# Threshold attention with a squared-ReLU layer: squares of the first chunk on VectorE, its values in another PSUM bank, query copies a step earlier

## The chip, the cores and the metric

The kernel runs on one core of a Trainium2 chip. The metric is the device time in microseconds (us) of one execution, as the median of several runs. Five engines work side by side, each through its own queue in order: TensorE (PE, with its weight loads PEld), VectorE (DVE), ScalarE (ACT), GpSimd (POOL) and SyncE (SP), which here only issues DMAs. Semaphores order them against each other.

## What is computed

```python
scores = scale * np.matmul(q, k.transpose(0, 1, 3, 2))       # 8 batches x 8 heads, 576 x 576, head_dim 64
thresh = np.max(scores, axis=-1, keepdims=True) - tau
scores = np.where(scores >= thresh, scores, -1000000000.0)
attn = np.exp(scores - np.max(scores, axis=-1, keepdims=True))
attn = attn / (np.sum(attn, axis=-1, keepdims=True) + 1e-09)
x = np.matmul(attn, v)                                       # to (4608, 512), heads side by side
h = x @ w_in                                                 # (512, 2048)
r = np.maximum(h, 0.0)
out = (r * r) @ w_out                                        # (2048, 512)
```

Everything is fp32.

## The kernel before

**Visits and steps.** The attention is done by pairs of heads. A visit is a pair's walk over blocks of 128 query rows, one block to a step; the last block has only 64 rows, and its two heads lie side by side in one tile (`qmid`). The first batch is walked twice: visits 0 to 3 take blocks 0 and 1, visits 4 to 7 take blocks 2, 3 and 4, so that the first 256 tokens are complete early. Later visits take all five blocks.

In a step, TensorE makes scores into PSUM banks 0 to 3 (L280, for the last block L273 from `qmid`). VectorE takes row maxima (L317); ScalarE makes the bias and threshold (L340, L341) and the exponents (L343); VectorE applies the threshold and sums (L355), then makes a reciprocal (L359, L360); GpSimd divides (L365, L367). Two steps later TensorE transposes the weights (L414, L421, L427) in parts 0, 1 and 2, each into one of banks 4 and 5 in turn (`take("tx", (4, 5))`), and ScalarE copies them to `wT` (L415, L423, L428). Values are then made by `mix` (L530, from `wT` and `vs`, 20 matmul records), also into a bank of 4 and 5, and copied to `xT` (L513). At a visit's last step VectorE transposes the next visit's queries and keys (L254). `split_left` (L248) copies the last 64 queries of both heads into `qmid` on ScalarE: two copies of 64x64.

**Rounding of weights.** The weights of the second part arrive by DMA in 32 pieces of 128x512. Each piece passes through five instructions in stages: L149 and L150 on ScalarE, L152 and L154 on VectorE (integer `tensor_scalar`), L156 and then L158 on GpSimd, which writes the finished piece to `w_in_sb` or `wo` and lets the next load start (L136). This is spread over the steps up to about 200 us: one piece in most steps, two in a few.

**The second part.** Tokens are taken in chunks of 256. Chunk 0 is done plainly (`PLAIN = 1`): 16 pieces `mlp_in` (L577), two of which share a PSUM bank, and then `mlp_out` (L759). Later chunks use a scheme with fewer products (`product`, L794, and `unit`, L688). For the first layer of chunk 0, `take("mm", (6, 7))` gives banks 6 and 7 in turn, one to each pair of pieces. After a pair, `square` runs: ScalarE's relu from PSUM to `g` (L587), and GpSimd's multiplication of `g` by itself (L588).

**Order of the work.** Each engine's order is written out by the kernel's Python loop, not by a scheduler. `waiting` is the queue of pieces of the second part; `fill` puts as many into each quarter of a step as `rate` allots in estimated us, and `after` runs what a piece left to be done (`posts`) one or two calls later. Steps before `early_to` go through `early_step`; the steps around the change go through the loop at L1186 to L1294; there `split_left(n)` stands at L1231, in the visit's second step (`at == 1`), after the exponents. Its copies are read by the scores of the visit's last step. The 8 squares of chunk 0 run between 60 and 136 us, during visits 5 to 8. For visits 5 to 7 the three steps are here called first, second and third (blocks 2, 3 and 4).

```python
        if s in mixes and old:
            mix(*mixes[s])
...
        if old:
            turn(*old, 2)()
```

So values are made after parts 0 and 1 of the transposes, and part 2 comes after the values.

Of the kernel before, what the change touches and what calls it, by code (L numbers as in the profile page):

```python
# [12 lines left out]
ALU = mybir.AluOpType  # L13
# [6 lines left out]
def kernel(  # L20
# [10 lines left out]
    nc = tc.nc  # L31
# [14 lines left out]
    PLAIN, SEVEN = 1, 2  # L46
# [34 lines left out]
    at = RAW * 2 * WP  # L81
# [127 lines left out]
    def arrived(t):  # L209
        assert all(x[0].tensor.name != t.tensor.name for x in loads)  # L210
# [163 lines left out]
    def take(what, among):  # L374
        used[what] += 1
        at = among[used[what] % len(among)]
        if what == "mm":
            last_used(at)
        return bank[at]
# [8 lines left out]
    def last_used(x):  # L388
        oldest.remove(x)
        oldest.append(x)  # L390
# [10 lines left out]
    def place_of(n, i):  # L401

        return n % 2 * 4 + 2 * i if n < HP else n % 2 * 5 + 2 * (i - FIRST) if n < 2 * HP else 2 * i
# [123 lines left out]
    def mix(n, cols):  # L527

        def term(ps, u, c, at, rows=slice(0, P), first=False, last=False):
            nc.tensor.matmul(ps[u * D:(u + 1) * D, :], vs[n % 2][rows, u * (NBLK + 1) + c, :],  # L530
                             wT[rows, at // REST:(at + ps.shape[1]) // REST, NBLK if c == NBLK else u * (NBLK + 1) + c, :],
                             start=first, stop=last)

        above, below = slice(0, D), slice(D, P)
        arrived(vs[n % 2])
        if not by_dma(n):
            ps = take("tx", (4, 5, 6, 7) if early() else (4, 5))[:, 0:cols.stop - cols.start]
            at = place_of(n, cols.start // P) * REST
            for c in range(NBLK + 1):
                for u in range(2):  # L540
                    term(ps, u, c, at, first=(c == 0), last=(c == NBLK))
            put(n, cols.start, ps, False)
            return
        n1, n2 = 2 * P + REST, 2 * P
        at = ODD if paired(n) and n % 2 else ONE
        one, two = bank[0], bank[4]
        groups = (one[:, 0:n1], at, (above, below)), (two[:, 0:n2], TWO, (below, above))
        for ps, x, _ in groups:
            for c in range(NBLK):
                for u in range(2):  # L550
                    term(ps, u, c, x, first=(c == 0))

        for ps, x, places in groups:
            for u, rows in enumerate(places):
                term(ps, u, NBLK, x, rows, last=True)
        put(n, 0, one[:, ONE - at:ONE - at + 2 * P], True)
        left = ODD if at == ODD else LEFT - at
        put(n, NBLK * P, one[:, left:left + REST], False)
        put(n, 2 * P, two[:, 0:n2], True)
# [10 lines left out]
    def mlp_in(j, x):  # L570

        f, at = FORDER[x], j * TCH % RING
        if x % 2 == 0:
            used["h"] = take("mm", (6, 7)) if j < PLAIN else next_bank()
        h = used["h"].rearrange("p (f n) -> p f n", f=2)
        for c in range(NMC):
            nc.tensor.matmul(h[:, x % 2, :], w_in_sb[:, c, f * P:(f + 1) * P], xT[:, c, at:at + TCH],  # L577
                             start=(c == 0), stop=(c == NMC - 1))
        if x == NFT - 1:
            read_to["x"] = (j + 1) * TCH  # L580
            if j == SEVEN - 1:
                ask(*((j, "S3", q, c) for q in range(2) for c in range(2)))
        posts = [lambda: some_sums(1)] if j >= PLAIN else []
        if x % 2:
            def square():
                to = g[:, f - 1:f + 1, :]
                nc.scalar.activation(out=to, in_=h, func=AF.Relu)  # L587
                nc.gpsimd.tensor_tensor(out=to, in0=to, in1=to, op=ALU.mult)  # L588
                if j >= PLAIN and x % 8 == 7:
                    square_half(x // 8 * (HF // 2))  # L590
            posts.append(square)
        return posts
# [252 lines left out]
    def paired(n):  # L845

        return n >= 3 * HP
# [7 lines left out]
    def by_dma(n):  # L855

        return n >= 3 * HP - 1
# [7 lines left out]
    for s, (n, i) in enumerate(steps):  # L865
# [5 lines left out]
        if i in mixed:  # L871
            first, lag = mixed[i]
            cols = slice(first * P, S if by_dma(n) else min((i + 1) * P, S))
# [6 lines left out]
    chunk_at, j = {}, 0  # L880
# [9 lines left out]
    waiting = deque()  # L890
    state = {"us": 0.0, "left": 0.0, "step": 0, "free": False, "rounded": 0, "usable": 0, "then": [], "last": [], "made": 0}

    def early():
        return state["step"] < early_to
# [46 lines left out]
    def after():  # L941
        now = state["last"]
        state["last"] = []
        for fn in state["then"]:
            state["last"] += fn() or []
        state["then"] = []
        for fn in now:
            fn()
# [237 lines left out]
    for s in range(END + 1):  # L1186
        state["step"] = s
        if early():
            rounded_by.append(state["rounded"])
            done += pieces[s]  # L1190
            early_step(s)
            continue
        if s >= first_late:
            assert 4 not in kept.values()
            late_step(s)
            continue
        state["usable"] = rounded_by[-1]
        rounded_by.append(state["rounded"])
        on = s < NST
        now = []  # L1200
        if on:
            n, i = steps[s]
            at = visits[n][1].index(i)
            last = at == len(visits[n][1]) - 1
            now = list(range(done, done + pieces[s]))
            done += pieces[s]
            more = n + 1 < len(visits)
            short = n < 2 * HP
            if short and at == 0 and 0 < n + 1 < 2 * HP:
                load_qk(n + 2)  # L1210
            elif not short and at == 1 and not by_dma(n):
                load_qk(n + 1)
            if now:
                round_weights(now[0], 0)
            scores(s)()
            after()
            some_later("gpsimd")
        old = steps[s - 2] if 2 <= s < NST + 2 and not by_dma(steps[s - 2][0]) else None
        at_once = now or old
        lay = on and last and more and not by_dma(n)  # L1220
        if old:
            turn(*old, 0)()
            turn(*old, 1)()
        if on:
            exponents(n, i)
            if s and by_dma(steps[s - 1][0]):
                turn_last(s)
            for p in now[1:]:
                round_weights(p, 0)
            if at == 1:  # L1230
                split_left(n)  # L1231
            if lay:
                prep(n + 1)
            elif now:
                round_weights(now[0], 1)
        if s in mixes and not old:
            mix(*mixes[s])
            for j in chunk_at.get(s, ()):
                add_chunk(j)
        quarter = rate(s) / 4 if s < END else 1e9  # L1240
        fill(quarter)
        if s in mixes and old:
            mix(*mixes[s])
            for j in chunk_at.get(s, ()):
                add_chunk(j)
        if old:
            turn(*old, 2)()
        state["free"] = s > first_dma
        smooth = s > first_dma + 2 and s not in mixes
        some_later("vector")  # L1250
        some_later("gpsimd")
        if smooth:
            after()
        if on:
            threshold(n, i)
            for fn in prep_at[s] + load_at[s]:
                fn()
            if lay and now:
                round_weights(now[0], 1)
            if now:  # L1260
                round_weights(now[0], 2)
                round_weights(now[0], 3)
            for p in now[1:]:
                assert not lay
                round_weights(p, 1)
                round_weights(p, 2)
                round_weights(p, 3)
            if not at_once:
                divide(n, i)
        if smooth:  # L1270
            fill(quarter)
            after()
            some_later("gpsimd")
        for what in place_at[s]:
            place_blocks(*what)
        some_loads()
        some_later("vector")
        if not smooth:
            some_later("gpsimd")
            fill(quarter)  # L1280
        some_loads()
        if on and at_once:
            divide(n, i)
        fill(quarter)
        some_loads()
        fill(quarter)
        some_loads()
        if on:
            for p in now:
                end_rounding(p)  # L1290
            if at == 0 and 0 < n <= 2 * HP:
                load_v(n)
            elif last and n >= 2 * HP and not by_dma(n):
                load_v(n + 1)  # L1294
# [35 lines left out]
```

## Time and profile before

| | |
|---|---|
| median of 3 runs | 1323.08 us (1322.36 to 1323.74) |
| the profiled execution's own time | 1322.66 us |
| its span, first to last instruction | 1320.9 us |
| mean granted TensorE clock | 0.998 |
| L588, GpSimd's squares of chunk 0 | 8 of 1.03 to 1.23 us, 70.1 to 132.2 us |
| L587, relu of chunk 0 | 8 of 0.57 to 0.62 us, 64.9 to 125.8 us |
| L152 and L154, rounding on VectorE | 32 each, 0.41 to 1.51 us |
| L355, threshold on VectorE | 269 of 0.81 us on average |
| L248, copies to `qmid` | 16 of 0.23 to 0.26 us |
| TensorE idle, 60 to 136 us | 5.0 of 76 us |

In the lines of the profile, `out<-in` names the tiles, followed by shape and type, `xN` counts instructions, and in the timeline a bracket gives the time that the engine sat idle before the instruction and what ended it. "Busy" counts from the start of an instruction to its end, whatever it waits for in between. The chain of work that ended last is followed back from the last instruction, at each step to what released it. A wait is put down to the event that came last.

### The profile page before, as it was taken

What the parts mean: (1) busy time and instruction counts of PE and PEld (TensorE: products, weight loads), DVE (VectorE), ACT (ScalarE), POOL (GpSimd) and SP (SyncE); (2) the same over time, 40 slices, a digit from 0 to 9 for tenths busy, and PEclk for the clock granted to TensorE, in tenths of its full rate; (3) what the DMA queues carried; (4) which work ended last, traced back from release to release, by engine and by line L of the source; (5) the groups of instructions that cost most, each with busy time, mean ns of one, the idle gap of its engine ahead of it and who ended that gap; (6) DMA issues with size and microseconds to landing.
All of it is one profiled execution on the core that took longest, in us unless ns stands there. A gap on an engine that the chain in (4) does not pass through costs nothing.

```text
span 1320.9 us, 24730 instructions
## 1 busy us (share of the span) xinstructions
PE 1291.0 (98%) x8862; PEld 1069.3 (81%) x8862; DVE 941.8 (71%) x2026; ACT 583.8 (44%) x1353; POOL 785.8 (59%) x916
## 2 busy tenths in 40 slices
PE   7999999999999999999999999999999999999998
PEld 6666557887887888797878888888887988889997
DVE  6899876787777878788776877878686877622131
ACT  4878773334353526253535343534353434331331
POOL 3799874774747465556564655656574737454351
PEclk9999999999999999999999999999999999999999
DMA  6765531676786878686666768657676866520000
GB/s 128 160 162 144 141 69 62 139 180 163 161 184 165 186 167 203 137 200 163 165 150 165 160 156 188 173 126 185 149 179 138 196 161 164 144 53 9 9 17 17
DMA packets 320907, 185.48 MB, mean 140 GB/s; under 512 B 282224, under 2 KB 282256, under 8 KB 314384
## 3 DMA queue, kind: packets, MB, share of 16 engines
q1 hardware_dynamic: 309120, 115.78, 46.3%
q0 software_dynamic: 10000, 67.92, 12.8%
q8 instruction: 70, 1.15, 0.4%
q14 instruction: 53, 0.43, 0.1%
q10 hardware_dynamic: 1664, 0.21, 0.1%
HBM read 108.04 MB, written 68.42 MB: 134 GB/s over the span
## 4 chain that ended last, share of the span: by engine, by line
PE 84%; DVE 5%; DMA 3%; ACT 2%; POOL 1%; issue 1%; SPq 0%; DVEq 0%; POOLq 0%
PE big L688 29%; PE big L794 28%; PE big L530 10%; PE big L296 8%; PE big L577 4%; PE big L280 2%; PE big L759 2%; DMA wT<-aside 1%; DMA aside<-turned 1%; PE big L414 1%; DVE w L355 1%; DVE st L317 1%; ACT w L343 1%; DVE turned L154 0%; POOL w_in_sb L158 0%
## 5 line engine op out<-in xcount | busy, mean ns | idle before, releaser
L355 DVE SCALAR_TENSOR_TENSOR w<-big,st,w 128x576 f32<-128x576 f32 x269 | 207.8, 807 | 87.2 <-ACT w L343 85.3
L317 DVE TENSOR_REDUCE st<-big 128x1 f32<-128x576 f32 x288 | 204.2, 748 | 83.4 <-PE big L296 61.4
L367 POOL TENSOR_SCALAR w<-w,st 128x576 f32<-128x576 f32 x269 | 243.8, 915 | 29.4 <-DVE st L360 24.7
L794 PE MATMUL big<-wo,gsum 128*128 128x256 f32 x1088 | 243.8, 382 | 0.0
L794 PEld LDWEIGHTS big<-wo,gsum 128*128 128x128 f32 x1088 | 204.4, 190 | 37.0 <-issue 7.6
L688 PE MATMUL big<-xT,w_in_sb 128*128 128x128 f32 x1536 | 187.4, 277 | 1.5 <-DVE g L700 1.4
L688 PEld LDWEIGHTS big<-xT,w_in_sb 128*128 128x128 f32 x1536 | 178.5, 192 | 10.7 <-issue 7.7
L794 PE MATMUL big<-wo,g 128*128 128x256 f32 x816 | 185.3, 382 | 0.1
L343 ACT ACTIVATE w<-big,st 128x576 f32<-128x576 f32 x255 | 174.1, 733 | 0.2 <-issue 0.2
L794 PEld LDWEIGHTS big<-wo,g 128*128 128x128 f32 x816 | 151.6, 190 | 26.1 <-issue 6.5
L530 PE MATMUL big<-wT,vs 128*64 128x320 f32 (+5 forms) x1420 | 159.7, 389 | 6.7 <-DMA wT<-aside 3.3
L530 PEld LDWEIGHTS big<-wT,vs 128*64 128x64 f32 (+1 forms) x1420 | 85.5, 136 | 72.8 <-issue 20.2
L340 ACT ACTIVATE st<-st 128x2 f32<-128x2 f32 (+1 forms) x137 | 27.9, 203 | 256.0 <-DVE st L317 255.0
L365 POOL TENSOR_SCALAR st<-st 128x2 f32<-128x2 f32 (+1 forms) x148 | 35.8, 242 | 176.6 <-DVE w L355 166.0
L436 POOL DMA_DIRECT2D aside<-turned x50 | 29.9, 597 | 177.8 <-DVE turned L465 177.8
L700 DVE TENSOR_TENSOR g<-big,g 128x512 f32<-128x512 f32 x96 | 64.8, 677 | 83.4 <-PE big L688 77.8
L296 PE MATMUL big<-kT,qT 64*128 64x256 f32 (+3 forms) x768 | 107.0, 416 | 0.0
L296 PEld LDWEIGHTS big<-kT,qT 64*128 64x128 f32 x768 | 84.5, 186 | 14.5 <-issue 5.0
L696 ACT ACTIVATE g<-g 128x512 f32<-128x512 f32 x96 | 60.3, 628 | 63.8 <-DVE g L700 63.7
L567 POOL TENSOR_TENSOR gsum<-g 128x512 f32<-128x512 f32 x34 | 46.1, 1355 | 69.8 <-ACT g L697 60.2
L697 ACT ACTIVATE g<-g 128x512 f32<-128x512 f32 x128 | 80.7, 630 | 4.1
L459 DVE STREAM_TRANSPOSE turned<-w 128x512 f32<-128x512 f32 x100 | 70.3, 703 | 0.0
(118 smaller groups left out, 2070.0 us busy)
## 6 DMA issues: line engine op xcount, KB each, us to landing
aside<-turned POOLq DMA_DIRECT2D x50, 1152.0 KB, 4.8
wT<-aside SPq DMA_DIRECT2D x200, 288.0 KB, 5.4
vs<-in_v_dram SPq DMA_DIRECT2D x72, 128.0 KB, 5.8
wo<-in_moe_w_in_dram SPq DMA_DIRECT2D x16, 512.0 KB, 4.8
wo<-in_moe_w_out_dram SPq DMA_DIRECT2D x16, 512.0 KB, 3.6
out_dram<-osb POOLq DMA_DIRECT2D x32, 256.0 KB, 4.2
kl<-in_k_dram SPq DMA_DIRECT2D x113, 72.0 KB, 3.3
ql<-in_q_dram SPq DMA_DIRECT2D x112, 72.0 KB, 5.7
```

The source lines that it names most:

```text
L296: nc.tensor.matmul(big[to, at + x0:at + x1], lhsT, keys[u * D:(u + 1) * D, x0:x1], start=True, stop=True)
L317: nc.vector.tensor_reduce(out=mx[:, u:u + 1], in_=sc[u], axis=AX.XY, op=ALU.max)
L343: nc.scalar.activation(out=w[:, u, :].rearrange("p (h k) -> p h k", h=2), in_=sc[u], func=AF.Exp, bias=bias[:, u:u + 1], scale=SCALE)
L355: nc.vector.scalar_tensor_tensor(out=wu, in0=sc[u], scalar=thr[:, u:u + 1], in1=wu, op0=ALU.is_ge, op1=ALU.mult, accum_out=sm[:, u:u + 1])
L367: nc.gpsimd.tensor_scalar(out=w[:, u, :], in0=w[:, u, :], scalar1=z[:, u:u + 1], scalar2=rcp[:, u:u + 1], op0=ALU.add, op1=ALU.mult)
L459: move(wb[:, 0:h, :, :], whole_[:, 0, :, :, :])
L530: nc.tensor.matmul(ps[u * D:(u + 1) * D, :], vs[n % 2][rows, u * (NBLK + 1) + c, :], wT[rows, at // REST:(at + ps.shape[1]) // REST, NBLK ...
L688: nc.tensor.matmul(to[:, f, :], factor(j, p, q, c)[:, f * P:(f + 1) * P], part[:, c, :], start=(p in "125" and f == 0 and c == 0), stop=(p ...
L696: nc.scalar.activation(out=to, in_=to if src is None else src, func=AF.Relu)
L697: nc.scalar.activation(out=to, in_=to, func=AF.Square)
L700: nc.vector.tensor_tensor(out=x, in0=to, in1=x, op=ALU.add)
L794: nc.tensor.matmul(to, left[:, f, :], wo[:, slot, f, :], start=(f == 0), stop=(f == HF - 1))
```

## The change

Three edits. The square of chunk 0 is made by VectorE: ScalarE's relu stays, and then max(h, 0) from PSUM times that relu is written in place. Values that are due when a pair of first-layer pieces of chunk 0 is next take a bank of 6 and 7 in turn with these pairs, not of 4 and 5. And `split_left` is called in a visit's first step.

```diff
@@ mix
-            ps = take("tx", (4, 5, 6, 7) if early() else (4, 5))[:, 0:cols.stop - cols.start]
+            plain = not early() and waiting and waiting[0][1] is mlp_in and waiting[0][2] < PLAIN and waiting[0][3] % 2 == 0
+            ps = take("mm", (6, 7)) if plain else take("tx", (4, 5, 6, 7) if early() else (4, 5))
+            ps = ps[:, 0:cols.stop - cols.start]
@@ mlp_in, square
                 nc.scalar.activation(out=to, in_=h, func=AF.Relu)
-                nc.gpsimd.tensor_tensor(out=to, in0=to, in1=to, op=ALU.mult)
+                if j < PLAIN:
+                    nc.vector.scalar_tensor_tensor(out=to, in0=h, scalar=0.0, in1=to, op0=ALU.max, op1=ALU.mult)
+                else:
+                    nc.gpsimd.tensor_tensor(out=to, in0=to, in1=to, op=ALU.mult)
@@ the loop over steps
-            if at == 1:
+            if at == 0:
                 split_left(n)
```

In the built program the order of TensorE and SyncE is the same as before. GpSimd's queue loses the 8 L588. VectorE's gains 8 instructions: in visits 5 to 7 one after the maxima of the second step, ahead of L152, and one after the maxima of the third step, ahead of the transposes L254; the last two stand after the maxima of the second and third step of visit 8. ScalarE's queue has the copies L248 a step earlier in visits 5 to 11, after the exponents and ahead of L415.

## The prediction, made before the changed kernel was run

> **What bounds the kernel now.** I read the page first, then the stretches of time, then the waits of TensorE, the chain that ended last, and the timeline of one visit, in that order. On the page TensorE leads by far:
>
> ```profile
> PE 1291.0 (98%) x8862; PEld 1069.3 (81%) x8862; DVE 941.8 (71%) x2026; ACT 583.8 (44%) x1353; POOL 785.8 (59%) x916
> ```
>
> But this is a mean over stages. All the squares of the first chunk run between 60 and 136 us. The stretches of time (columns: length, then busy us of PE, PEld, DVE, ACT, POOL with counts, clock, DMA) show that stage against the rest:
>
> ```profile
> 60.00:136.00 76.00, 71.03 (x425) 49.60 (x424) 73.29 (x130) 58.09 (x135) 70.22 (x72) 1.00 0.59 155
> 205.00:1320.90 1115.90, 1103.66 (x7657) 942.48 (x7656) 769.00 (x1671) 436.70 (x998) 628.88 (x727) 1.00 0.61 142
> ```
>
> Here VectorE is busy for 73.3 of 76 us and GpSimd for 70.2, while TensorE idles for 76.00 - 71.03 = 5.0 us. That 5.0 us is also the most that the change can win in this stage. The chain that ended last (start, length, what) runs through VectorE and GpSimd once in each visit:
>
> ```profile
> 109.30 1.39 DVE turned L154
> 110.87 1.29 issue
> 112.48 1.62 POOL w L367 x2
> 114.10 2.83 POOL w_in_sb L158 x2
> 116.97 0.70 PE big L577 x2
> ```
>
> One visit is three steps (i = 2, 3, 4; I call them first, second, third) and takes 18.73 us (the second step's row maxima L317 start at 102.20 and then at 120.93). Why VectorE is so full is seen in the timeline of the second and third step:
>
> ```profile
> 71.38 0.42 DVE L152 TENSOR_SCALAR turned<-turned 128x512 uint32<-128x512 uint32 x1
> ...
> 103.55 1.22 DVE L152 TENSOR_SCALAR turned<-turned 128x512 uint32<-128x512 uint32 x1
> ...
> 104.71 0.82 DVE L355 SCALAR_TENSOR_TENSOR w<-big,st,w 128x576 f32<-128x576 f32 x1
> ...
> 106.53 1.27 POOL L158 TENSOR_TENSOR w_in_sb<-turned 128x512 f32<-128x512 f32 x1
> 106.58 1.50 DVE L154 TENSOR_SCALAR turned<-turned 128x512 uint32<-128x512 uint32 x1
> ...
> 107.76 1.22 POOL L588 TENSOR_TENSOR g<-g 128x512 f32<-128x512 f32 x1
> ...
> 108.00 1.26 DVE L152 TENSOR_SCALAR turned<-turned 128x512 uint32<-128x512 uint32 x1
> ...
> 108.94 1.45 POOL L156 TENSOR_TENSOR turned<-turned 128x512 f32<-128x512 f32 x1
> ...
> 109.30 1.38 DVE L154 TENSOR_SCALAR turned<-turned 128x512 uint32<-128x512 uint32 x1
> ...
> 110.82 1.27 POOL L156 TENSOR_TENSOR turned<-turned 128x512 f32<-128x512 f32 x1 [0.43 <-DVE turned L154]
> ```
>
> L152 takes 0.42 us alone and 1.2 us when a GpSimd instruction is running: it ends 0.28 us after that instruction does (L588 ends at 108.98, L152 at 109.26). Most of VectorE's "busy" time here is standing in line.
>
> [...] L355 reads PSUM and one SBUF tile and lasts 0.77 to 0.82 us whatever GpSimd does. So the new square should not stand in that line. [...] The trace's nearest row, L700 (one PSUM, one SBUF operand, 512 elements), is 677 ns on the page.
>
> **The change, part by part.**
>
> *Removed from GpSimd:* 8 L588, 9.0 us in all (1.13 us mean, 1.03 us when not held up), two in each visit.
>
> *Added to VectorE:* 8 squares. Bounds: 0.65 us (L700's least) and 0.82 us (L355, which has 576 elements and an accumulator). I take 0.68; since neighbours overlap by some 0.07, each adds 0.63 to the queue: 5.0 us in all if nothing covered it. A cost below nothing is excluded for the instruction itself; what it frees is counted below.
>
> *One visit worked through* from the timeline, times from t0 = the start of the second step's maxima (102.20 in the trace), GpSimd's TENSOR_TENSOR at 1.27, L367 at 0.81:
> 1. Second step, behind the maxima. They end at 1.42; L355 can't start before 2.51, as it waits for ScalarE's exponents (L343). L152 now fills this with its stand in line. New: square 0.68 + L152 0.42 = 1.10 in a gap of 1.09. [...]
> 2. The run L154, L152, L154 that ends at 110.68, so at 8.48. New: the first L154 waits for L158 and ends near 5.30. The L588 that held the following L152 is gone and GpSimd now waits for L154's data, so L152 follows at once (5.65). GpSimd's L156 then runs to 6.82 and the last L154 ends at about 7.05. Gain 1.43.
> 3. Third step: L317, then the second square (+0.63), the transposes L254, L355, then L152 and L154. Counted from x = the end of that last L154: GpSimd does L156, L367 x2 and reaches its two L158 at x + 3.39 (before: 110.68 to 114.07, the same). L152 got in just ahead of them, at x + 3.02; it now comes at x + 3.65 (x + 3.51 in the two visits whose queries are short). So it stands behind the first L158 and L154 behind the second: L154 ends at x + 6.38, not x + 5.11. Loss 1.27.
> 4. First step: maxima, L152, L355 (again held to the exponents, 1.09 after the maxima), L154. The L588 at 116.89 that held L152 is gone, and GpSimd is through with its work when L154 comes. Maxima to next maxima: 5.22 before, 1.42 + 1.09 + 1.54 for two L355 + 0.4 for L359 and L360 + 0.35 = about 4.7. Gain 0.5.
> Sum of a visit: -1.43 + 1.27 - 0.5 = -0.66 us.
>
> *The visits.* The first (from 65.84) has no long stand in part 2, its L154 ending at 73.21 of which about 0.53 goes; it has the loss of part 3: -0.53 + 1.27 - 0.5 = +0.24. The next two give -0.66 each: -1.1 by 121 us. The last two squares (to 136) have parts 1 and 2 without the transposes of part 3, but TensorE's own queue (L280 at 132.67) limits what is won to about 0.9. Sum -2.0 us.
>
> *Values in a bank of the first layer.* TensorE waits 2.0 us in four places for ScalarE's copies L415 ahead of the values L530, since both share banks 4 and 5. Three of the four go to banks 6 and 7 (at 127.63 no first-layer piece is next). But the wait after it, L280 for L355 (1.1 us), ends when VectorE is ready, not TensorE: up to 0.66 us each of TensorE is freed, and spent there. Counted at 0; if VectorE were the early one it would be worth up to 1.8. The bank is now held until VectorE's square instead of ScalarE's relu: the square ends near 104.3 for the pair from 101.0, the values use the bank at 109.4; the next pair comes to the other bank at 115.2 against a square at about 112. No wait.
>
> *Last queries copied in the first step.* 14 copies L248 (0.24 us, two in each of visits 5 to 11) move ahead on ScalarE's queue past L415, L149, L150, the relu and L423 of the first step, each of which is 0.48 later; the next exponents wait for maxima anyway (ScalarE idles 0.57 there). They issue no DMA and pass no queue but ScalarE's. Gone is TensorE's wait for them (0.4 us in two places), and in the second step L149 and L150 come 0.48 earlier, which part 2 needs: its L152 at 5.2 finds L149 done at about 5.1, not 5.6. Alone 0.
>
> *New wait:* the square waits for ScalarE's relu L587; L152, the transposes and L355 are queued behind it, and L280 behind those. The relu ends at 102.07 and 109.02, the square comes at 103.6 and about 109.8, so it waits for nothing; a relu 0.8 us later would be felt one for one.
>
> *Rest of the program.* After 205 us TensorE is busy for 1103.7 of 1115.9 us in an order that doesn't change, so an earlier start is kept one for one. Against its own time the profiled execution goes from 1322.66 (span 1320.9) to 1320.7; that execution lies 0.4 below the median, so on the median 1323.08 - 2.0 = 1321.1.
>
> **Rivals.**
> A (my forecast): part 3 gives back most of part 2. 1321.1, own range 1319.8 to 1322.6.
> B: L152 still slips in ahead of the first L158 in the third step. It needs only 0.12 to 0.26 us; the square at 0.65 and a later L367 would do it. For it: L152 at 67.18 got in though L367 had started 0.14 before. Against: at 106.53 GpSimd won with a lead of 0.05. Then a visit wins about 1.1, the values' bank begins to count, and the total is 3 x 1.1 + 0.9 = 4.2, near the ceiling of 5.0: 1318.9.
> C, slower: the squares aren't hidden on VectorE, and the engine that is 96% busy becomes the bound. Place: the third step, ahead of the transposes and L355, for which TensorE's L280 already waits. If the first L588's going brings less in part 2 than part 3 costs (the point is 1.27 - 0.5 = 0.77 of gain there; L149 arriving late behind the moved copies would do it), each visit loses: with 0 in part 2 it is 3 x 0.77 + 0.3 = 2.6: 1325.7.
> D: the squares aren't on the path at all, and the gain is given back at the next common wait between 136 and 205, where TensorE idles for another 69.00 - 66.73 = 2.3 us: 1323.
>
> **Chances.** A 0.50, B 0.28, C 0.14, D 0.08. The likeliest is A: 1321.1. The range takes in B at 1318.9 and half of C: 1318.4 to 1324.6. What a measurement can tell from no change is about 0.2%, 2.6 us: faster means under 1320.4, which is B and a fifth of A, 0.38; slower means over 1325.7, half of C and a little for an unseen wait, 0.09; the rest 0.53.
>
> **What would show it.** Right: no L588 before 136; squares near 0.68; the L152 after the first L154 at 0.42 to 0.6, not 1.26; L152 and L154 of the third step at 1.1 to 1.4 each; no wait of L530 for L415 in three visits, more wait of L280 for L355; visits of 18.0 to 18.1. B shows in an L152 of 0.42 in the third step and visits under 17.8. C shows in visits of 19 us or more. The forecast is wrong if the square proves longer when GpSimd runs, or if the chain leaves VectorE and GpSimd.

## The result, and the profile after

The changed kernel takes 1319.66 us as a median (1318.06 to 1321.79) against 1323.06 us before (1321.97 to 1324.35, 9 runs each): ratio 0.9976, 95% interval 0.9967 to 0.9985. That is 3.4 us less (2.0 to 4.4): no change lies outside that interval, and the difference is barely above the 0.2% that the prediction took for what a measurement can tell. The forecast was 2.0 us less.

The page's first line of the changed kernel, and the two stretches of time that answer to those of before (columns as there):

```profile
PE 1290.9 (98%) x8862; PEld 1070.6 (81%) x8862; DVE 936.9 (71%) x2034; ACT 585.4 (44%) x1353; POOL 776.2 (59%) x908
```

```profile
60.00:136.00 76.00, 72.91 (x433) 51.33 (x432) 70.97 (x142) 60.66 (x142) 65.06 (x69) 1.00 0.60 158
205.00:1319.10 1114.10, 1101.59 (x7648) 941.32 (x7646) 768.28 (x1668) 436.45 (x994) 628.27 (x727) 1.00 0.61 142
```

TensorE idles for 3.1 us between 60 and 136 us, no longer 5.0. VectorE has more instructions and is busy for less time: 71.0 us, not 73.3. Its L152 and L154 take 28.0 us of that, before 36.4. Unheld, each takes 0.41 us; by that estimate they stand in line for 14.1 us, before for 22.8. The timeline of the same visit as before, second and third step:

```profile
100.68 1.42 DVE L317 TENSOR_REDUCE st<-big 128x1 f32<-128x576 f32 x2
...
105.06 0.92 DVE L154 TENSOR_SCALAR turned<-turned 128x512 uint32<-128x512 uint32 x1
...
105.90 0.41 DVE L152 TENSOR_SCALAR turned<-turned 128x512 uint32<-128x512 uint32 x1
...
106.35 1.38 DVE L154 TENSOR_SCALAR turned<-turned 128x512 uint32<-128x512 uint32 x1
...
108.32 0.68 DVE L591 SCALAR_TENSOR_TENSOR g<-big,g 128x512 f32<-128x512 f32 x1
...
111.13 2.68 POOL L158 TENSOR_TENSOR w_in_sb<-turned 128x512 f32<-128x512 f32 x2
...
111.36 1.32 DVE L152 TENSOR_SCALAR turned<-turned 128x512 uint32<-128x512 uint32 x1
...
112.72 1.38 DVE L154 TENSOR_SCALAR turned<-turned 128x512 uint32<-128x512 uint32 x1
```

The run L154, L152, L154 now ends at 107.73, 7.05 us after the second step's maxima (L317 at 100.68); before it took 8.48. The square (L591 in this kernel) takes 0.67 to 0.68 us in all eight places, whatever GpSimd does. In the third step of this visit L152 comes 0.23 us after GpSimd's L158 and stands in line, and L154 behind the second L158. One visit earlier it went the other way:

```profile
93.72 0.41 DVE L152 TENSOR_SCALAR turned<-turned 128x512 uint32<-128x512 uint32 x1
93.77 2.90 POOL L158 TENSOR_TENSOR w_in_sb<-turned 128x512 f32<-128x512 f32 x2
```

L152 started 0.05 us ahead of L158 and took 0.41 us. Which of the two starts first is called the *race* below. The chain that ended last, over the stretch of the first of these two timelines, is put down to VectorE alone, no longer to GpSimd's L158:

```profile
106.35 0.63 DVE turned L154
107.28 0.37 issue
107.66 0.75 DVE st L317
108.40 0.60 DVE g L591
...
111.44 1.25 DVE turned L152
```

The square itself (L591, 0.60 us) now lies on it. The 1.25 us of L152 are for the most part its stand behind L158. And TensorE's waits between 60 and 136 us (total, times, longest), first before, then after:

```profile
PE big L530 <- ACT wT L415: 2.0, 4, 0.7
PE big L280 <- DVE wo L355: 1.1, 2, 0.6
...
PE big L273 <- ACT qmid L248: 0.4, 2, 0.2
```

```profile
PE big L280 <- DVE wo L355: 1.5, 2, 0.9
...
PE big L280 <- DVE w L355: 0.5, 1, 0.5
...
PE big L530 <- ACT wT L415: 0.2, 1, 0.2
```

The values' wait for L415 fell from 2.0 to 0.2 us, the wait for the query copies is gone, and the waits of L280 for L355 rose from 1.1 to 2.0.

**Two measures for what follows.** A *visit* is the time from the second step's maxima to those of the next visit; for visits 5, 6 and 7 that was 17.63, 18.73, 18.73. The *stage* is the time from the 13th to the 61st sum that L355 writes out on VectorE (38.9 and 194.2 us in the profile of before); it is given as a difference to before. It leaves out two things that differ from one execution to the next whatever the kernel: when the stage is entered (-0.6 to +1.6 us over the 13 profiles), and whether the last values wait for their DMA. That wait is 1.4 us in the profile of before (it ends near 1164 us, the only TensorE wait listed from 1100 to 1300 us), 1.6 in the first profile after, and absent in the second. Over all 13 profiles, nine have it (1.1 to 1.6 us) and four don't: again and third_only, but also bank_copies and both_squares, where GpSimd still makes its squares. In the profile of before:

```profile
PE big L530 <- DMA wT<-aside: 1.4, 1, 1.4
```

Between the stage and there the shift moves by at most 0.6 us in any profile. Where the profiled executions' times differ by more than the stage does, it is mostly these two.

| kernel | ratio to before, 95% interval | visits 5, 6, 7 | stage |
|---|---|---|---|
| changed, first | 0.9976 (0.9967 to 0.9985) | 16.87, 17.36, 18.25 | -2.5 |
| again | 0.9975 (0.9966 to 0.9985) | 16.85, 17.36, 18.26 | -2.5 |
| sq_alone | 0.9982 (0.9975 to 0.9989) | 17.42, 17.39, 17.76 | -2.4 |
| bank_copies | 0.9997 (0.9988 to 1.0005) | 17.63, 18.72, 19.9* | +0.8* |
| third_only | 0.9988 (0.9980 to 0.9996) | 17.69, 18.01, 18.90 | -0.4 |
| second_only | 0.9975 (0.9964 to 0.9986) | 16.82, 17.90, 17.90 | -2.65 |
| third_halves | 0.9986 (0.9978 to 0.9994) | 18.61*, 17.98, 17.98 | +0.85* |
| both_squares | 1.0001 (0.9993 to 1.0009) | 17.65, 20.3*, 18.6* | +1.5* |
| no_square | 0.9965 (0.9951 to 0.9979) | 16.82, 17.12, 17.11 | -4.1 |
| square_late | 0.9968 (0.9956 to 0.9979) | 17.64*, 17.31, 17.32 | -1.65* |
| square_late_2 | 0.9967 (0.9954 to 0.9979) | 16.82, 17.31, 17.32 | -3.7 |
| third_on_scalar | 0.9971 (0.9961 to 0.9981) | 16.81, 17.26, 17.27 | -3.85 |

(* TensorE ran at half its clock for 3.4 us in this profile, in that visit or the stretch just ahead of it; see the last section. Such a visit or stage can't be compared: square_late's visit 5 is 0.8 us longer than that of square_late_2, the same kernel, and its stage 2.1 us.)

### The profile page after: what moved, and what is told of

Read it like the earlier page. It is cut to its first block, busy times and chain, and to the rows that moved or that the text cites. A ratio compares the mean times of both kernels' runs of the same rounds, so it can differ in the third digit from the quotient of the medians.

```text
span 1319.1 us, 24730 instructions
## 1 busy us (share of the span) xinstructions
PE 1290.9 (98%) x8862; PEld 1070.6 (81%) x8862; DVE 936.9 (71%) x2034; ACT 585.4 (44%) x1353; POOL 776.2 (59%) x908
## 4 chain that ended last, share of the span: by engine, by line
PE 83%; DVE 6%; DMA 3%; ACT 2%; issue 1%; POOL 1%; SPq 0%; DVEq 0%; POOLq 0%; ACTq 0%
PE big L693 29%; PE big L799 28%; PE big L530 10%; PE big L296 8%; PE big L579 3%; PE big L764 2%; PE big L280 2%; DVE st L317 1%; DMA wT<-aside 1%; DMA aside<-turned 1%; PE big L414 1%; DVE w L355 1%; ACT w L343 1%; DVE turned L154 0%; PE big L273 0%
## 5 line engine op out<-in xcount | busy, mean ns | idle before, releaser
L355 DVE SCALAR_TENSOR_TENSOR w<-big,st,w 128x576 f32<-128x576 f32 x269 | 207.4, 805 | 87.6 <-ACT w L343 85.6
L317 DVE TENSOR_REDUCE st<-big 128x1 f32<-128x576 f32 x288 | 204.1, 747 | 85.3 <-PE big L296 60.6
L367 POOL TENSOR_SCALAR w<-w,st 128x576 f32<-128x576 f32 x269 | 244.2, 916 | 29.4 <-DVE st L360 24.6
L530 PE MATMUL big<-wT,vs 128*64 128x256 f32 (+5 forms) x1420 | 159.5, 389 | 4.9 <-DMA wT<-aside 3.5
L530 PEld LDWEIGHTS big<-wT,vs 128*64 128x64 f32 (+1 forms) x1420 | 86.0, 136 | 70.1 <-issue 20.8
L340 ACT ACTIVATE st<-st 128x2 f32<-128x2 f32 (+1 forms) x137 | 28.1, 205 | 253.3 <-DVE st L317 252.1
```

The costliest lines, as they stand in the source:

```text
L317: nc.vector.tensor_reduce(out=mx[:, u:u + 1], in_=sc[u], axis=AX.XY, op=ALU.max)
L355: nc.vector.scalar_tensor_tensor(out=wu, in0=sc[u], scalar=thr[:, u:u + 1], in1=wu, op0=ALU.is_ge, op1=ALU.mult, accum_out=sm[:, u:u + 1])
L367: nc.gpsimd.tensor_scalar(out=w[:, u, :], in0=w[:, u, :], scalar1=z[:, u:u + 1], scalar2=rcp[:, u:u + 1], op0=ALU.add, op1=ALU.mult)
```

## Which part of the change is it?

The edits shown from here on are against the changed kernel. Theory 1: GpSimd's squares held up VectorE's L152 and L154, which take 0.41 us unheld and up to 1.51 us beside GpSimd's work (profile of before); their going is the gain, and VectorE's squares cost what a lost race in the third step costs. Theory 2: the gain is TensorE's waits that the bank and the copies take away.

**again**: the changed kernel unaltered.

> The changed kernel once more, beside its variants. The profile of it shows 3.4 us won between 60 and 136 us, with two visits of -0.8 and -1.4 us in which L152 of the third step got ahead of GpSimd's L158, and one of -0.5 us in which it didn't. Theory 1 [...]: 3.4 us faster than before, 1319.7, and a spread of some 1 us from run to run, as the race at L158 falls one way or the other. Theory 2 (the gain comes from TensorE's waits that the bank and the copies remove): the same total, without a link to that race.

Measured 0.9975, and in the profile the same three visits to 0.02 us, with the race won in visits 5 and 6 and lost in 7 as before. So in these two profiles the race falls the same way, and what sets the two apart lies elsewhere. The part of the expectation that laid the spread to the race has no support. The 3.4 us that it puts between 60 and 136 us are how far VectorE's maxima moved there; about 1 us of that is lost again in waits for TensorE (see the account of the rest, below), and the stage holds 2.5. What differs between the two profiles is the entry (1.02 against 0.57 us late) and the last values' wait (0 against 1.6).

**sq_alone**:

```diff
-            ps = take("mm", (6, 7)) if plain else take("tx", ...)
+            ps = take("tx", (4, 5, 6, 7) if early() else (4, 5))
-            if at == 0:
+            if at == 1:
                 split_left(n)
```

> Only the square on VectorE; values in banks 4 and 5 and query copies in the second step as before. Theory 1: most of the gain, -2.5 us (1320.6); of the 3.4 some 0.3 a visit is lost because ScalarE's L149 comes 0.48 later behind the copies, so that L152 after the first L154 falls behind GpSimd's L156 (1.2 us long in place of 0.41). Theory 2: at most -1.0, as TensorE still waits 2.0 us for L415 and 0.4 for L248.

Measured 0.9982, 2.4 us less, which is theory 1's number; the stage is -2.4, as with the whole change. But the reason given for the missing part is not in the trace: L152 after the first L154 takes 0.42 us here too, at 88.07, before the L149 next to it even begins (88.26). It doesn't need that L149, but the pair before. The sum is the same by another road: in visit 6 the run L154, L152, L154 ends 6.55 us after the maxima, earlier than in the changed kernel (7.05), and the next first step takes 5.75 us from maxima to maxima, not 5.22.

**bank_copies**: the other two edits without the square.

```diff
-                if j < PLAIN:
-                    nc.vector.scalar_tensor_tensor(out=to, in0=h, scalar=0.0, in1=to, op0=ALU.max, op1=ALU.mult)
-                else:
-                    nc.gpsimd.tensor_tensor(out=to, in0=to, in1=to, op=ALU.mult)
+                nc.gpsimd.tensor_tensor(out=to, in0=to, in1=to, op=ALU.mult)
```

> The bank of the values and the place of the copies changed, the square left on GpSimd. Theory 1: 0 to -0.6 us, since the wait of L280 for L355 takes up what TensorE gains. Theory 2: -2.4 us, the waits of L530 for L415 (2.0) and of L273 for L248 (0.4).

Measured 0.9997: nothing (1.6 us less to 0.7 more). In its profile the wait of L530 for L415 is down to 0.2 us and that of L280 for L355 up to 3.9:

```profile
PE big L280 <- DVE wo L355: 3.9, 3, 1.8
```

What TensorE wins it waits off one matmul group later. Theory 2 falls. With the square there, the two edits move the stage from -2.4 to -2.5; the medians of 0.9982 and 0.9976 can't be told apart.

## Which of the two squares of a visit?

**third_only** and **second_only** leave one of the two squares of each visit on GpSimd:

```diff
-                if j < PLAIN:
+                if j < PLAIN and x % 4 == 3:        # third_only; x % 4 == 1 in second_only
                     nc.vector.scalar_tensor_tensor(out=to, in0=h, scalar=0.0, in1=to, op0=ALU.max, op1=ALU.mult)
```

> VectorE takes only the squares of the third step; those of the second step stay on GpSimd, where they hold L152 between the two L154. Theory 1: no gain in the run L154, L152, L154, loss of the race in the third step, some of it given back in the first step, where GpSimd's square is gone: +0.8 a visit, +1.5 to +2.5 in all against before. If the gain came simply from less work on GpSimd: half of it, -1.7.

> VectorE takes only the squares of the second step; those of the third step stay on GpSimd, where they run in the next first step. Theory 1: the gain of the run L154, L152, L154 is there in part (GpSimd still has one square a visit, which keeps its queue about 0.8 later than in the changed kernel), and there is no square ahead of the third step's L152, so the race is won in all visits: -0.8 to -1.2 a visit, -2.5 us in all (1320.4). If the third step's square were free, it would be less than half of the changed kernel's gain, -1.5.

third_only was forecast slower and is faster or equal: its median is 1.6 us less (0.5 to 2.6), which is the number of the other guess, less work on GpSimd (-1.7), but its stage holds only -0.4. second_only has all of the gain (0.9975, stage -2.65), although it moves only half of the squares. The timelines of visit 6 show why the first forecast failed. In second_only:

```profile
87.66 1.28 POOL L158 TENSOR_TENSOR w_in_sb<-turned 128x512 f32<-128x512 f32 x1
87.72 1.52 DVE L154 TENSOR_SCALAR turned<-turned 128x512 uint32<-128x512 uint32 x1
...
89.15 0.41 DVE L152 TENSOR_SCALAR turned<-turned 128x512 uint32<-128x512 uint32 x1
...
93.86 0.83 DVE L152 TENSOR_SCALAR turned<-turned 128x512 uint32<-128x512 uint32 x1
94.38 2.85 POOL L158 TENSOR_TENSOR w_in_sb<-turned 128x512 f32<-128x512 f32 x2
```

In third_only, the run's first L154:

```profile
86.55 1.28 POOL L158 TENSOR_TENSOR w_in_sb<-turned 128x512 f32<-128x512 f32 x1
...
87.40 0.71 DVE L154 TENSOR_SCALAR turned<-turned 128x512 uint32<-128x512 uint32 x1
```

The run L154, L152, L154 ends 7.65 us after the maxima in second_only and 7.70 in third_only, 8.48 before and 7.05 in the changed kernel. So in visits 6 and 7 each square's going brings about half of it, in a way of its own. With the second step's square gone, the L152 between is 0.41, not 1.26. With the third step's gone (1.04 us, in the next first step), GpSimd's whole queue is 0.8 us earlier, L158 is nearly through when the first L154 comes, and that L154 takes 0.71 us, not 1.50. What I had not counted is that work on an engine's queue acts wherever that engine is next waited for. The third step's square gives its half back where it makes L152 lose the race, as it stands on VectorE ahead of that: third_only's visit 6, with the race won, is 0.72 us shorter than before, and visit 7, with the race lost, 0.17 longer.

## The race in the third step

**third_halves**: the same square as two instructions.

```diff
-                    nc.vector.scalar_tensor_tensor(out=to, in0=h, scalar=0.0, in1=to, op0=ALU.max, op1=ALU.mult)
+                    for part in ((0, 1) if x % 4 == 3 else (slice(0, 2),)):
+                        nc.vector.scalar_tensor_tensor(out=to[:, part], in0=h[:, part], scalar=0.0, in1=to[:, part], op0=ALU.max, op1=ALU.mult)
```

> The changed kernel with the third step's square as two instructions of 256 elements: a little longer (some 0.2 to 0.25 us), the same work. Theory 1 (race): L152 was ahead of L158 by only 0.05 in visits 5 and 6, so it now loses in all visits and each of the two is 0.9 longer: +1.8 against the changed kernel, -1.6 against before. Without a race: the added length alone, 3 x 0.22 = +0.7 against the changed kernel at most.

Two halves follow each other so closely that they add only 0.06 us. That was enough:

```profile
96.64 2.68 POOL L158 TENSOR_TENSOR w_in_sb<-turned 128x512 f32<-128x512 f32 x2
96.66 1.54 DVE L152 TENSOR_SCALAR turned<-turned 128x512 uint32<-128x512 uint32 x1
```

Being 0.02 us behind GpSimd's L158, L152 takes 1.54 us; being 0.05 ahead, it took 0.41. Visit 6 is 17.98 us in place of 17.36: 0.06 us of added work cost 0.62. The medians are 1.3 to 1.5 us slower than the changed kernel's (0.9986 against 0.9976 and 0.9975; forecast 1.8); their intervals overlap, so it is the visits that show the loss. Visit 5 follows a stretch at half clock, but from its third step's maxima on it is 0.88 us longer than in the changed kernel; visit 7, where the race is lost in both, is 0.27 shorter. Together that is 1.2 us, where added work of 0.06 a visit would come to 0.2. The forecast of 0.9 a visit (1.2 for the race, 0.3 given back in the next first step, where L152 then takes 0.44 and L154 0.41) left out that GpSimd is then also earlier at the run L154, L152, L154, which ends 6.77 us after the maxima and not 7.05.

Between the two outcomes, 0.41 and 1.54 us, lie 0.07 us in the order of the starts.

## What do VectorE's squares cost, and what is left?

**no_square**:

```diff
-                    nc.vector.scalar_tensor_tensor(out=to, in0=h, scalar=0.0, in1=to, op0=ALU.max, op1=ALU.mult)
+                    pass
```

> The changed kernel without any square of chunk 0: neither GpSimd nor VectorE multiplies, g keeps the relu, so the first 256 tokens come out as relu(h) @ w_out. It prices what GpSimd's squares cost, alone. Theory 1 [...]: all of the gain and no loss of the race in the third step: -4.5 us against before, as with the square between L152 and L154. Rival C (VectorE's squares are on the path at their whole length): the changed kernel's 3.4 plus 8 x 0.63 = 5.0, so -6 us or more.

Measured 0.9965, stage -4.1. By the stage, VectorE's eight squares cost 4.1 - 2.5 = 1.6 us of their 8 x 0.63 = 5.0 us, 1.1 of it in visit 7 (17.11 against 18.25), where the race is lost. The median's own interval (2.8 to 6.5 us less) would let Rival C's -6 stand; the stage and the next experiment rule out its price of 5.0.

**both_squares**: VectorE's instructions as dummies, GpSimd's squares back in place (the constant tile is set once, at the start).

```diff
-                    nc.vector.scalar_tensor_tensor(out=to, in0=h, scalar=0.0, in1=to, op0=ALU.max, op1=ALU.mult)
-                else:
+                    nc.vector.scalar_tensor_tensor(out=osb[:, 0, :]..., in0=h, scalar=0.0, in1=osb[:, 1, :]..., op0=ALU.max, op1=ALU.mult)
+                if True:
                     nc.gpsimd.tensor_tensor(out=to, in0=to, in1=to, op=ALU.mult)
```

> The changed kernel with GpSimd's squares put back, and VectorE's 8 instructions left in as dummies of the same shape (PSUM and a constant tile into a tile not yet in use). It prices VectorE's additions with nothing freed on GpSimd. Theory 1: in the second step they are hidden in a wait (0); in the third step L152 comes after GpSimd's first L158 in all three visits, which costs up to 1.27 each: +2.5 us against before (1325.0). If they cost nothing: 0. If they cost their whole length: +5.

Measured 1.0001: nothing (0.9 us less to 1.2 more), against 2.5 us expected. Visit 5 is 17.65, as before (17.63). L152 won the race in visits 5 and 6 (0.41 us both) and lost it in 7, so one of the three losses that I had counted came. Its stage and its later visits can't be read, as TensorE ran slow in visit 6.

**square_late** (and once more as **square_late_2**) puts the third step's square between L152 and L154:

```diff
                 if j < PLAIN:
-                    nc.vector.scalar_tensor_tensor(...)
+                    def on_vector():
+                        nc.vector.scalar_tensor_tensor(...)
+                    if x % 4 == 3 and x < NFT - 1:
+                        put_off.append(on_vector)
+                    else:
+                        on_vector()
...
             if lay and now:
                 round_weights(now[0], 1)
+                while put_off:
+                    put_off.pop()()
```

> As the changed kernel, but in the third step of visits 5 to 7 the square stands between L152 and L154, where VectorE waits for GpSimd's first L158 anyway, and no longer ahead of the transposes and L355. Theory 1: L152 comes 0.63 earlier and is ahead of L158 in every visit, the square costs nothing there; the visit that lost the race wins another 1.2: -4.5 us against before (1318.6). If the square ahead of the transposes cost nothing (rival), the same as the changed kernel, -3.4 us.

> The version with the third step's square between L152 and L154 once more; its profile before fell on an execution in which TensorE ran at half its clock for some 3 us at 59 us, which hid what the visits won. Theory 1: 1.0 less than the changed kernel, 1318.2, with three visits of 17.3 and a stage (39 to 194 us) 3.3 shorter than before.

Measured 0.9968 and 0.9967. Of the second forecast, two visits are as named (17.31, 17.32) and the first is shorter (16.82). The third step of visit 6 in the second of them:

```profile
91.97 0.84 DVE L152 TENSOR_SCALAR turned<-turned 128x512 uint32<-128x512 uint32 x1
92.50 2.85 POOL L158 TENSOR_TENSOR w_in_sb<-turned 128x512 f32<-128x512 f32 x2
92.73 0.67 DVE L594 SCALAR_TENSOR_TENSOR g<-big,g 128x512 f32<-128x512 f32 x1
...
93.33 0.89 DVE L154 TENSOR_SCALAR turned<-turned 128x512 uint32<-128x512 uint32 x1
```

L152 is half a microsecond ahead of L158 (it stands behind L367 and ends 0.28 us after it), the square runs while L154 would stand behind L158 anyway, and L154 takes 0.89 us in place of the 1.37 that it takes in second_only. From the third step's maxima to the next maxima it takes 5.12 us, in no_square 5.13: the square costs nothing there. The stage is -3.7, 0.4 from the kernel without any square; what is left is the second step's square (see part 1 below).

**third_on_scalar** gives the third step's square to ScalarE:

```diff
-                if j < PLAIN:
+                if j < PLAIN and x % 4 == 3:
+                    nc.scalar.activation(out=to, in_=to, func=AF.Square)
+                elif j < PLAIN:
                     nc.vector.scalar_tensor_tensor(...)
```

> The second step's square on VectorE, the third step's on ScalarE (Square, after its relu), which idles there before the next exponents. Theory 1: VectorE's third step is then as short as without any square and GpSimd is free of both: nearly all that the kernel without squares won (its stage was 4.1 shorter), -4.3 us against before (1318.5). If ScalarE's extra 0.63 delays its copies L415 and the next L340, no better than the changed kernel, -3.4.

Measured 0.9971, stage -3.85. ScalarE does it in 0.63 us and its copies L415 still end ahead of the next L340. By the stage both this version and square_late_2 win 1.2 to 1.35 us over the changed kernel, and both beat the kernel before. Their medians' intervals overlap with that of the changed kernel, so only the profile shows them ahead of it.

## Why the prediction was right, and where it was off

The mechanism and the sign were right: the gain is VectorE's stand in line behind GpSimd's squares; the L152 between the two L154 of visit 7 took 1.26 us before and 0.41 after. (The prediction called most of VectorE's busy time there such a stand; by the estimate above it is 22.8 of 73.3 us between 60 and 136 us, under a third.) Of the measured 3.4 us the stage holds 2.5; the forecast's sum was 2.0. The stage's 2.5 lies inside the interval of 2.0 to 4.4, so the other 0.9 us may be no more than the medians' spread. Whether the change also acts on the last values' wait is open: one profile of before and two after (1.4; 1.6 and 0) can't say it, and the wait is absent in two kernels that keep GpSimd's squares too.

The sum agrees less well by its terms (forecast, measured): visit 5 +0.24, -0.76; visit 6 -0.66, -1.37; visit 7 -0.66, -0.48; the rest -0.9, +0.1. The visits won 1.5 us more than forecast and the rest 1.0 less, so that the sum came within 0.5 us is in part luck.

- *Part 1* (behind the maxima, 1.10 us in a gap of 1.09): right for VectorE itself; L355 waits for ScalarE's exponents for another 0.16 us even with square and L152 in the gap. But it costs part 2 some 0.2 us: behind the square, L152 starts when L367 has just started and delays it: the two L367 take 1.90 us in visit 6, 1.63 in no_square. L158 is later by that, and the run of part 2 ends after 7.05 us, not 6.84.
- *Part 2* (7.05 forecast, 7.05 measured in visits 6 and 7): right as a sum, wrong in its parts. I put all of it on the L588 between; the other one has half, by way of GpSimd's queue.
- *Part 3* (race lost everywhere, +1.27): the step that failed. In visit 7 L154 ended at x + 6.37, forecast x + 6.38. In visits 5 and 6 L152 came at x + 3.36, not x + 3.51, against L158 at x + 3.41, so the race was won, and the step cost 0.06 us (to the next maxima) and not 1.27: rival B there, A in visit 7. The 0.15 are the square's spacing (0.60, not 0.63) and L355: before, it was held by the exponents that came after the transposes, so a little of the square was hidden in that.
- *Part 4* (-0.5; its own numbers add up to 4.8, which is -0.4): right only where the race was lost (visit 7 -0.31; third_halves -0.3). Where L152 wins it, GpSimd is through with its two L158 0.22 us later (the pair takes 2.90 us in visit 6, 2.68 in visit 7), L152 of the first step takes 1.39 us behind L156, and the time from first to second maxima is 5.22 as before. Parts 3 and 4 are one account: what the race takes, the next step gives back in part.
- *The rest* (-0.9): wrong. VectorE's marks in visit 8 did come early (L317 at 132.25, 2.8 us less than before), but TensorE's queue was the bound, as the forecast had it in words: L280 there came only 1.7 earlier, and L273 too. VectorE's lead was lost waiting.
- *Bank and copies* (0): right in sum (sq_alone, bank_copies). The remark that part 2 needs the earlier L149 was wrong.
- *Rival C* did not come: VectorE's instructions alone cost nothing that can be measured (both_squares), and 1.6 us by the stage beside no_square.
- *Rival D* (all given back by 205 us) did not come either: counted from the start of each profile, VectorE is 2.0 us ahead of before at the end of visit 7, 2.8 at 132 us and still 1.9 at 192 us.
- *No change after 205 us*: right; TensorE's busy time from there is 1101.6 of 1114.1 us, and the shift stays.

## What to carry to other kernels

An instruction's recorded time can be mostly its place in line behind another engine (VectorE's L152 beside GpSimd's work: 0.41 to 1.54 us here). Find by the timeline which starts first (L152 took 0.41 us when it started 0.05 us ahead of L158, 1.54 when 0.02 behind), and when a forecast hangs on a margin of 0.1 us, give neither side more than even odds, even if the same side then wins in every execution, as in the two profiled here. Work taken from an engine's queue can pay at every later place where that engine is waited for, not only where the instruction stood (in third_only a later L154 took 0.71 us, not 1.50). Put what doesn't stand in that line (the square took 0.67 us with GpSimd's L158 under way in square_late_2) into the time in which the engine stands waiting in it, not ahead of the race.

## What was not expected of the hardware

Between 55 and 140 us, TensorE's granted clock fell to half for 3.4 us in four of the thirteen profiles, each time 0.3 to 1.3 us after the end of an idle time of 1.75 to 2.2 us. In square_late (columns as in the stretches above; the clock is third from the end):

```profile
57.00:59.00 2.00, 0.26 (x6) 0.02 (x2) 1.07 (x4) 1.92 (x6) 2.00 (x3) 1.00 0.83 273
59.00:60.00 1.00, 0.98 (x6) 0.78 (x8) 0.97 (x2) 1.00 (x4) 0.92 (x2) 0.67 0.82 272
60.00:61.00 1.00, 1.00 (x7) 0.24 (x3) 0.97 (x3) 0.47 (x1) 0.89 (x2) 0.50 1.16 248
```

TensorE had waited for L355 for 1.76 us; the L280 at 59.02 then took 2.02 us instead of 1.24, and the visit's first step 6.71 instead of 5.43. The same wait of 1.72 to 1.78 us stands in every other profile at that place; the clock fell there in third_halves too, and in the other eleven nothing followed. So the idle time alone doesn't decide it, and that these idle times caused the falls is not shown.
